# A fourth outer product done as inner products, in three of four pairs of the second matrix chain's first layer

## The chip, the core and the metric

The kernel runs on one core of one Trainium2 chip. The metric is the device time of one execution in microseconds (us); three runs of the kernel before gave 853.53, 854.23 and 855.94. A core has five engines that each work through their own list of instructions in order and wait for one another by semaphores: TensorE (PE in the profile; its weight loads are listed apart as PEld), VectorE (DVE), ScalarE (ACT), GpSimd (POOL) and SyncE (SP). SP, ACT and POOL also issue the transfers from and to memory. Matrix products land in PSUM, eight banks of 128 partitions by 512 fp32 columns; everything else is kept in SBUF.

## What is computed

```python
mask   = q_bucket[:, :, :, None] == k_bucket[:, :, None, :]      # 6 sign bits of q @ proj, k @ proj
scores = np.where(mask, scale * q @ k.T, -1e9)
x      = softmax(scores) @ v          # 4 batches x 8 heads x 768 x 64, laid out as 3072 x 512
h      = x @ w_in                     # 512 x 2048, "first layer"
g      = np.maximum(h, 0) ** 2        # gate
out    = g @ w_out                    # 2048 x 512, "second layer"; all fp32
```

## The kernel before

The attention comes first and fills `x` in memory (the first layer starts at 313.6 us in the trace). Then 3072 tokens go through the two layers in three chunks of 1024 (`i` = 0, 1, 2). For each chunk the *hidden stage* makes the gated hidden units and `project(i)` makes the output (the *output stage*). The order of all instructions is written out by hand (`tc.manual_schedule()`): what the code calls first stands first in each engine's queue.

Both layers use Strassen's scheme with seven products in place of eight (Winograd's form, with sums shared). `product` is one such level: `at(0..6)` are the seven left factors, `bt` the right ones, and the results c11, c12, c21, c22 come out of running sums in PSUM: products 0, 4, 5 and 2 are added one after the other into the same bank `acc0`, and after each of the first three ScalarE copies the running sum out (`one`, `two`, `three`) before the next may be added. Product 1 goes to a second bank, 3 and 6 to a third.

In chunk 0 the first layer is one level: for each of eight row blocks `r` of 128 hidden units, seven products of 128x512. In chunks 1 and 2 it is two levels, done in *pairs*: blocks `r0 = n` and `r = NQ + n` (n = 0 to 3) are made by two calls of `hidden_pair` (`half` 0 and 1). Four of the seven outer products (0, 3, 4, 5) are done plainly in each half, 128x512 each and two matmuls per product, by `add` (L1204 to L1210). The other three (1, 2, 6) are split once more: over the pair each is a set of seven inner products of 128x256, one matmul each. `inner_steps` gives such a set as four steps plus `put`; the sets are called A, B and C, and a set serves both blocks of the pair. The calls of `hidden_pair` set the order in which outer products and inner steps stand on TensorE. The copies out of PSUM are ScalarE's (`keep`, L1214, and L1166 to L1189), the sums of inner results VectorE's (L1169, L1183, L1185), `put` adds the outer partial result and gates (L1193, L1019), and `gate_sum` makes b22. Every matmul is fp32 and stands as two instructions in the trace.

After a pair VectorE forms differences of its gated blocks (`minus`, L676, `inner_sums`), which the output stage reads. The output stage is seven calls of `product` (k = 0 to 6), each seven products of 128x256 with four matmuls.

Transfers: `load_unit` loads a half's weights (`w_unit`, two buffers, 512 KB, SP's queue) two halves ahead; `load_inner` loads the inner factors of the next pair; `load_leaf` the second layer's factors on ScalarE's queue. `load_x(i + 1)` (2 MB, POOL's queue) stands at the start of the output stage. On the side ScalarE squares the raw q and k in 32 pieces (`peak`, 128x768, with a running sum) for a guard on the size of the scores; `load_peak(i + 2)` on POOL's queue fetches a piece two ahead into two buffers. Before, all 32 squares stand in the hidden stages of chunks 1 and 2, two in each half (`mark`).

In PSUM, `ps_m` has three names with two buffers each (`acc0` to `acc2`) and `ps_t` one tile of two banks (`spare`); its halves serve as the third bank `last` of the inner sets. In SBUF there are five buffers `h` (`new_h`), one `five`, two `one`, one `two`, two `three`, and two `o`, into which the output stage writes its results.

Of the kernel before, what the change touches and what calls it, by code (L numbers as in the profile page):

```python
# [34 lines left out]
def kernel(  # L35
# [10 lines left out]
    nc = tc.nc  # L46
# [51 lines left out]
    p_i = fast.enter_context(tc.tile_pool(name="p_i", bufs=2, side="right"))  # L98
    ps_t = fast.enter_context(tc.tile_pool(name="ps_t", bufs=1, space=PSUM))
    ps_s = first.enter_context(tc.tile_pool(name="ps_s", bufs=2, space=PSUM))  # L100
# [621 lines left out]
    def load_unit(n, pool=p_i):  # L722

        if n < NCHUNK * NR and n not in w_unit:
            r = order(n)
            w_unit[n] = pool.tile([P, 7, NFT // 2, P], FP32, name="w_unit", bufs=2 if pool is p_i else 1)
            m = 7 if n < NR else 4
            nc.sync.dma_start(out=w_unit[n][:, 0:m], in_=w_in_7[r, :, 0:m])

    def sum_x(i, n):  # L730
# [6 lines left out]
    with tc.manual_schedule():  # L737
# [182 lines left out]
        p_r = fast.enter_context(tc.tile_pool(name="p_r", bufs=2, reuse_waits="tile"))  # L920
        p_k = fast.enter_context(tc.tile_pool(name="p_k", bufs=1, reuse_waits="tile"))
        ps_m = fast.enter_context(tc.tile_pool(name="ps_m", bufs=2, space=PSUM, reuse_waits="tile"))
        HN, QN, NH = NCH // 2, NCH // 4, 5

# [7 lines left out]

        def product(n, w, at, bt, c11, c12, c21, c22, hook=None, last=False):

# [51 lines left out]
        def peak(i):  # L986

            t = raw_qk.pop(i)
            nc.scalar.activation(out=t, in_=t, func=ACTF.Square, accum_out=peaks[:, i:i + 1])

        top = p_k.tile([P, 1], FP32, name="top2")

# [3 lines left out]
        def guard():  # L996

            tp = spare("tp")[:, 0]
# [54 lines left out]

        w_inner, t_inner, snaps, now = {}, {}, {}, {}

# [70 lines left out]
        def quarters_x(i, j):  # L1126

            x = xs[i][0]
            b = (x[:, 2:4, 0:HN], x[:, 0:2, HN:NCH], x[:, 2:4, HN:NCH])[j]
            return b[:, 0, 0:QN], b[:, 0, QN:HN], b[:, 1, 0:QN], b[:, 1, QN:HN]  # L1130

        def sums_inner(i, js):

            for j in js:
                t = p_y.tile([P, NQ, QN], FP32, name=f"t{j}", **({"bufs": 2} if j < 2 else {}))
                t_inner.setdefault(i, {})[j] = t
                y11, y12, y21, y22 = quarters_x(i, j)
                minus(t[:, 0], y12, y11)
                minus(t[:, 1], y22, t[:, 0])
                minus(t[:, 2], y21, t[:, 1])  # L1140
                minus(y12, y22, y12)

        def inner_steps(i, n, j):


            w, t = w_inner[i, n][j], t_inner[i][j]
            y11, t3, y21, y22 = quarters_x(i, j)
            hs = {}
            if i not in snaps:
                o = [p_y.tile([P, HN], FP32, name="o", bufs=NOUT) for _ in range(2)]  # L1150
                o = [o[m // 2][:, m % 2 * QN:(m % 2 + 1) * QN] for m in range(3)]
                snaps[i] = o, [t_inner[i][m][:, 3] for m in range(3)], spare("acc3")
            side = (3 * n + (0, 2, 1)[j]) % 2
            one, two, five = snaps[i][side]
            three = one
            last = snaps[i][2][:, side, 0:QN]

# [5 lines left out]
            def step_0():  # L1163
                a0, a1 = (ps_m.tile([P, 512], FP32, name=f"acc{m}")[:, 0:QN] for m in (1, 2))
                mul(a0, 0, y11, True, False)
                nc.scalar.copy(out=one, in_=a0)  # L1166
                mul(a1, 1, y21, True, True)
                hs[0] = new_h()
                nc.vector.tensor_tensor(out=hs[0][:, 0:QN], in0=a1, in1=one, op=ALU.add)  # L1169
                hs["a0"] = a0  # L1170

            def step_1():
                hs["a2"] = last
                mul(hs["a0"], 4, t[:, 1], False, False)
                nc.scalar.copy(out=two, in_=hs["a0"])
                mul(hs["a2"], 3, t[:, 0], True, False)
                nc.scalar.copy(out=five, in_=hs["a2"])

            def step_2():
                mul(hs["a0"], 5, t3, False, False)  # L1180
                nc.scalar.copy(out=three, in_=hs["a0"])
                mul(hs["a2"], 6, y22, False, True)
                nc.vector.tensor_tensor(out=hs[0][:, QN:HN], in0=hs["a2"], in1=two, op=ALU.add)  # L1183
                hs[1] = new_h()
                nc.vector.tensor_tensor(out=hs[1][:, QN:HN], in0=three, in1=five, op=ALU.add)  # L1185

            def step_3():
                mul(hs["a0"], 2, t[:, 2], False, True)
                nc.scalar.copy(out=hs[1][:, 0:QN], in_=hs["a0"])  # L1189

            def put(unit, out, other):
                h = hs[unit]
                nc.vector.tensor_tensor(out=h, in0=h, in1=other, op=ALU.add)  # L1193
                gated(out, h)

            return step_0, step_1, step_2, step_3, put

        def hidden_pair(i, n, half):

            r0, r = n, half * NQ + n  # L1200
            w, bt = w_unit.pop(i * NR + 2 * n + half), factors_x(i)
# [10 lines left out]
            def keep(of, name):  # L1212
                t = p_r.tile([P, 512], FP32, name=name, bufs=KEPT[name])
                nc.scalar.copy(out=t, in_=of)  # L1214
                return t

            def mark(m):
                peak(2 * ((i - 1) * NR + 2 * n + half) + m)

            if half == 0:  # L1220
                load_inner(i, n + 1)
                load_third_inner(i, n + 1, nc.sync)
                now["A"], now["C"], now["B"] = (inner_steps(i, n, j) for j in range(3))
            A, B, C = (now[c] for c in "ABC")
            add(acc, 0, "11", True, False)
            one = keep(acc, "one")
            if half == 0:
                A[0]()
            else:
                B[2]()  # L1230
                C[0]()
                A[4](1, b11[:, r], one)
                B[4](0, b12[:, r0], now["two"])
            mark(0)
            other = ps_m.tile([P, 512], FP32, name="acc2")
# [11 lines left out]
            if half == 0:  # L1247
                A[2]()
                B[0]()
                A[4](0, b11[:, r], one)  # L1250
                nc.vector.tensor_tensor(out=two, in0=two, in1=five, op=ALU.add)
            else:
                C[2]()
                nc.vector.tensor_tensor(out=two, in0=two, in1=five, op=ALU.add)
# [4 lines left out]
            mark(1)  # L1259
            add(acc, 5, "t3", False, True)  # L1260
# [46 lines left out]
        def add_to(out, one, two):  # L1307
            nc.vector.tensor_tensor(out=out, in0=one, in1=two, op=ALU.add)  # L1308

        def whole(one, two):  # L1310

            if two is None:
                return one
            t = p_y.tile([P, QN], FP32, name="tmp", bufs=2)
            add_to(t, one, two)
            return t

# [50 lines left out]
        def project(i):  # L1368

            V, W, U, X = (p_y.tile([P, 4, QN], FP32, name=f"sum{n}") for n in range(4))  # L1370
            outs = {}

# [54 lines left out]
            for k in range(7):  # L1427
# [23 lines left out]
                def hook():  # L1451
                    y21 = b[:, NQ:NR, 0:QN]
                    minus(y21, y21, t2)
                    if k > 1 and src:
                        factor_units(k - 1, src)
# [10 lines left out]
                def a_with_load(m, k=k):  # L1466
# [7 lines left out]
                    lambda p: use(2, p, None), lambda *p: use(3, *p), hook,  # L1474
                    (i, k) == (NCHUNK - 1, 6),
                )
# [60 lines left out]
        for i in range(NCHUNK):  # L1537
            for s in range(NR):
# [3 lines left out]
                else:  # L1542
                    hidden_pair(i, s // 2, s % 2)
                if i == 0:
# [18 lines left out]
                if i == 0:  # L1563
                    minus(b12[:, r], b22[:, r], b12[:, r])
                for n in range(2):
                    m = 2 * ((i - 1) * NR + s) + n
                    if 2 <= m + 2 < NPK:
                        load_peak(m + 2)
            if i == NCHUNK - 1:
# [215 lines left out]
```

## Time and profile before

| what | value |
|---|---|
| runs | 853.53, 854.23, 855.94 us; median 854.23 |
| profiled execution | 853.06 us, its span 851.5 us |
| PE busy | 846.1 us, 99% of the span |
| DVE, ACT, POOL busy | 746.2, 401.2, 167.8 us |
| TensorE clock granted | 0.999 of full |
| hidden stage of chunk 1 | 494.58 to 586.09 us, output stage to 670.70 us |
| hidden stage of chunk 2 | 670.70 to 762.21 us, output stage to the end |

The profile is one execution on the chip. "Busy" counts instructions, not waits; matmuls are pipelined, so the start of one instruction to the start of the next, not its listed duration, is what it costs TensorE. In a timeline row the first number is the start, the second the duration of the merged group, and brackets give the engine's idle time before it and who ended it. A row of stretches gives each engine's busy time and its number of instructions in a stretch.

### The profile page before, as it was taken

To read this page: it belongs to the slowest core of one execution; us is meant where nothing else is said; L and a number is where in the kernel's file an instruction comes from. 1 tells how busy PE (TensorE), PEld (TensorE's weight loads), DVE (VectorE), ACT (ScalarE), POOL (GpSimd) and SP (SyncE) were. 2 spreads that over 40 slices of the span, in tenths; PEclk is the share of its full clock that TensorE was granted. 3 is DMA by queue.
4 is the path that set the end of the run, shared out by engine and by line. 5 is a ranking of instruction groups with operands and counts; after the bars stand their busy time and mean duration, and the time that the engine had idled before them with its cause. 6 is when DMAs were issued, how large, how long until landed. Compare 5 with 4: busy or idle time off the path is not lost.

```text
span 851.5 us, 17019 instructions
## 1 busy us (share of the span) xinstructions
PE 846.1 (99%) x6594; PEld 532.4 (63%) x6594; DVE 746.2 (88%) x1023; ACT 401.2 (47%) x749; POOL 167.8 (20%) x283
## 2 busy tenths in 40 slices
PE   9999999999999999999999999999999999999998
PEld 4444444444465444444788866567888765668886
DVE  4898999999999988988999968888988788889777
ACT  5887777878777752222111145553111355541111
POOL 1321121303221201643122122221000311200003
PEclk9999999999999999999999999999999999999999
DMA  9966999989996517999977975527657865335467
GB/s 193 201 120 139 185 186 204 204 173 226 267 236 186 177 49 267 324 319 303 335 242 236 275 200 189 177 97 286 191 159 195 181 231 178 123 121 157 141 174 146
DMA packets 234229, 170.14 MB, mean 200 GB/s; under 512 B 164840, under 2 KB 193328, under 8 KB 234144
## 3 DMA queue, kind: packets, MB, share of 16 engines
q1 hardware_dynamic: 194384, 87.78, 42.3%
q0 software_dynamic: 16512, 42.45, 15.9%
q10 hardware_dynamic: 23248, 38.78, 14.6%
q8 instruction: 53, 0.87, 0.4%
q14 instruction: 32, 0.26, 0.1%
HBM read 127.15 MB, written 41.16 MB: 198 GB/s over the span
## 4 chain that ended last, share of the span: by engine, by line
PE 99%; ACT 0%; DVE 0%; issue 0%; POOL 0%; POOLq 0%
PE acc L942 41%; PE st L478 18%; PE xo L532 15%; PE acc L1206 13%; PE acc L1159 9%; PE tot L589 1%; PE hash L396 1%; PE tp L342 0%; PE xo L371 0%; PE hash L406 0%; PE xo L406 0%; ACT e L484 0%; PE acc L1358 0%; DVE o L1308 0%; ACT h L1360 0%
## 5 line engine op out<-in xcount | busy, mean ns | idle before, releaser
L484 ACT ACTIVATE e<-st 128x768 f32<-128x768 f32 x192 | 155.6, 811 | 56.0 <-PE st L478 51.8
L532 PE MATMUL xo<-e,v_nat 64*64 64x385 f32 (+1 forms) x1520 | 156.0, 483 | 0.0
L942 PE MATMUL acc<-b,leaf 128*128 128x256 f32 x600 | 133.0, 379 | 0.0
L942 PEld LDWEIGHTS acc<-b,leaf 128*128 128x128 f32 x600 | 113.8, 190 | 16.1 <-issue 0.5
L478 PE MATMUL st<-feat 64*64 64x384 f32 x1056 | 108.6, 482 | 0.0
L444 POOL DMA_DIRECT2D bits<-signed x120 | 62.1, 522 | 196.9 <-ACT signed L433 195.1
L532 PEld LDWEIGHTS xo<-e,v_nat 64*64 64x64 f32 (+1 forms) x1520 | 56.9, 133 | 67.3 <-issue 54.8
L1206 PE MATMUL acc<-t_x,w_unit 128*128 128x512 f32 x192 | 90.8, 595 | 0.0
L942 PE MATMUL acc<-t,leaf 128*128 128x256 f32 x336 | 76.0, 379 | 0.0
L942 PEld LDWEIGHTS acc<-t,leaf 128*128 128x128 f32 x336 | 63.8, 190 | 8.9 <-issue 0.3
L1019 DVE SCALAR_TENSOR_TENSOR b<-h 128x512 f32<-128x512 f32 x96 | 65.7, 691 | 3.0
L478 PE MATMUL st<-bits 64*64 64x384 bf16 x768 | 65.2, 324 | 0.0
L520 DVE TENSOR_TENSOR total<-total,e 128x1536 f32<-128x1536 f32 x32 | 56.0, 1750 | 7.6 <-ACT e L484 6.8
L520 DVE TENSOR_TENSOR t_x<-t_x,e 128x1536 f32<-128x1536 f32 x32 | 55.7, 1742 | 3.9 <-ACT e L484 3.8
L942 PE MATMUL acc<-x,w_unit 128*128 128x512 f32 x128 | 56.5, 593 | 0.0
L478 PEld LDWEIGHTS st<-feat 64*64 64x64 f32 x1056 | 39.0, 133 | 26.4 <-issue 21.7
L949 ACT COPY two<-acc 128x256 f32<-128x256 f32 (+1 forms) x29 | 12.5, 431 | 88.0 <-PE acc L942 78.6
L942 PE MATMUL acc<-b_t,leaf 128*128 128x256 f32 x240 | 53.8, 379 | 0.0
L1206 PEld LDWEIGHTS acc<-t_x,w_unit 128*128 128x128 f32 x192 | 35.8, 190 | 26.7 <-issue 23.0
L1327 POOL DMA_DIRECT2D out_dram<-h x24 | 15.5, 655 | 181.5 <-DVE h L1322 181.5
L942 PEld LDWEIGHTS acc<-b_t,leaf 128*128 128x128 f32 x240 | 45.6, 190 | 6.2
L949 ACT COPY one<-acc 128x256 f32<-128x256 f32 (+1 forms) x29 | 12.5, 431 | 77.6 <-PE acc L942 58.4
(192 smaller groups left out, 1379.2 us busy)
## 6 DMA issues: line engine op xcount, KB each, us to landing
leaf<-w_out ACTq DMA_DIRECT2D x142, 256.0 KB, 3.1
raw<-in_moe_w_in_dram SPq DMA_DIRECT2D x8, 1024.0 KB, 6.4
raw<-in_moe_w_out_dram SPq DMA_DIRECT2D x8, 1024.0 KB, 7.4
w_unit<-w_in SPq DMA_DIRECT2D x16, 512.0 KB, 4.0
w_unit<-w_in SPq DMA_DIRECT2D x8, 896.0 KB, 8.9
w_out<-sums POOLq DMA_DIRECT2D x16, 448.0 KB, 7.7
v_nat<-in_v_dram SPq DMA_DIRECT2D x16, 384.0 KB, 5.1
x_all<-x_raw SPq DMA_DIRECT2D x16, 384.0 KB, 3.2
```

The source lines that it names most:

```text
L396: nc.tensor.matmul(out=banks[g * NR_B:(g + 1) * NR_B, h, 0:HS], lhsT=projs[rows, h * D:h * D + NR_B], rhs=feat[pr][rows, w, c * HS:(c + 1) ...
L444: nc.gpsimd.dma_start(out=t[h * D:h * D + NBITS + 1, w, c * HS:(c + 1) * HS], in_=signed[pr % 2][at:at + NBITS + 1, h],)
L478: nc.tensor.matmul(out=st[k * HK:(k + 1) * HK, h, 0:HS], lhsT=src[1][rows, key], rhs=src[0][rows, cut], start=first, stop=not first, skip_ ...
L484: nc.scalar.activation(out=key_of(pr, kt)[:, :, i, 0:HS], in_=st[:, :, 0:HS], func=ACTF.Exp, scale=scale)
L520: nc.vector.tensor_tensor(out=totals[pr], in0=totals[pr], in1=e, op=ALU.add)
L532: return nc.tensor.matmul(out=outs[pr][h * D:(h + 1) * D, c, 0:HS + 1], lhsT=nat[pr, "v_nat"][rows, h, kt * D:(kt + 1) * D], rhs=key_of(pr ...
L942: nc.tensor.matmul(out=acc[to], lhsT=a(i), rhs=b(i), start=first and i == 0, stop=last and i == n - 1, skip_group_check=True,)
L949: nc.scalar.copy(out=t, in_=acc[of])
L1019: nc.vector.scalar_tensor_tensor(out=out, in0=h, scalar=0.0, in1=h, op0=ALU.max, op1=ALU.mult)
L1159: nc.tensor.matmul(out=out, lhsT=w(a), rhs=b, start=start, stop=stop, skip_group_check=True)
L1206: nc.tensor.matmul(out=to, lhsT=w[:, PLACE[a], f], rhs=bt[b](f), start=first and f == 0, stop=last and f == NFT // 2 - 1, skip_group_check ...
L1327: queue.dma_start(out=out[at, m0 + a * 32:m0 + (a + 1) * 32].rearrange("(c i) j -> i c j", i=32), in_=ot[a * 32:(a + 1) * 32].rearrange("i ...
```

## The change

In the pairs n = 0, 1, 2 of chunks 1 and 2 `hidden_wide` takes the place of `hidden_pair`: outer product 3 ("t1") is no longer two outer products but a fourth inner set D. Its right side is `t_x[0]`, whose four sums are made once per chunk into the two buffers `o`; three of its seven left factors are loaded with the unit of the pair's first half (slot 4 gets a second, 128 KB load) and four are made from them by VectorE in slots 5 and 6 (`sum_unit`). D's results for the two blocks (`fives`) are added to `two` and `three`. ScalarE now writes inner partial sums straight into `h`, and VectorE adds to them there (`adds`). b22 is added by VectorE and gated by ScalarE in two passes (Relu, Square: `gate_b22`). The second block's share of a pair's closing work (`rest`) is put off into the next pair's first half. The pair n = 3 keeps `hidden_pair`, with the new inner steps. `last` has two tiles of one bank each (`side_bank`); `ps_t` is closed with the attention's pools. `two` of the first half and the output stage's two `tmp` share one tile. The squares stand 9 in the hidden stage of chunk 1, 14 in its output stage (two per `product`, in `hook` and `beside`) and 9 in the hidden stage of chunk 2.

```diff
@@ load_unit
             nc.sync.dma_start(out=w_unit[n][:, 0:m], in_=w_in_7[r, :, 0:m])
+            if wide(n):
+                nc.sync.dma_start(out=w_unit[n][:, 4], in_=w_in_7[NQ + r, :, PLACE[3]])
+    def wide(n):
+        return n >= NR and n % 2 == 0 and n % NR // 2 < NQ - 1
+    def own_factors(w):
+        a = PLACE[3]
+        return (w[:, a, 0], w[:, a, 1], w[:, 4, 1]) + tuple(w[:, 5 + n // 2, n % 2] for n in range(4))
+    def sum_unit(n):
+        if n < NCHUNK * NR and wide(n):
+            w = w_unit[n]
+            a11, a12, a22, *to = own_factors(w)
+            sums_a(a11, a12, w[:, 4, 0], a22, *to)
@@ product
             three = keep(0, "three")
+            if beside:
+                beside()
             add(2, at(6), bt["22"], False, True)
@@ inner_steps
             def step_1():
-                hs["a2"] = last
-                mul(hs["a0"], 4, t[:, 1], False, False)
-                nc.scalar.copy(out=two, in_=hs["a0"])
-                mul(hs["a2"], 3, t[:, 0], True, False)
-                nc.scalar.copy(out=five, in_=hs["a2"])
+                mul(hs["a0"], 4, t2, False, False)
+                nc.scalar.copy(out=hs[0][:, QN:HN], in_=hs["a0"])
+                mul(last, 3, t1, True, False)
+                hs[1] = new(1)
+                nc.scalar.copy(out=hs[1][:, QN:HN], in_=last)
             def step_2():
...
-                nc.vector.tensor_tensor(out=hs[0][:, QN:HN], in0=hs["a2"], in1=two, op=ALU.add)
-                hs[1] = new_h()
-                nc.vector.tensor_tensor(out=hs[1][:, QN:HN], in0=three, in1=five, op=ALU.add)
+            def adds():
+                for unit, by in (0, last), (1, three):
+                    add_in(hs[unit][:, QN:HN], by)
+        def gate_b22(r):
+            nc.scalar.activation(out=b22[:, r], in_=b22[:, r], func=ACTF.Relu)
+            nc.scalar.activation(out=b22[:, r], in_=b22[:, r], func=ACTF.Square)
+        def hidden_wide(i, n, half):
...
+            add(acc, 0, "11", True, False)
+            one = keep(acc, "one")
+            if half == 0:
+                A[0]()
+                D[0]()
+                for step in behind_pair:
+                    step()
+                behind_pair.clear()
+            else:
+                B, C = inner_steps(i, 2, 0, w_inner[i, n][2]), inner_steps(i, 1, 1, w_inner[i, n][1])
+                B[0]()
+                C[0]()
+                B[1]()
+                gate_b22(r0)
+                A[4](1, b11[:, r], one)
+                sum_unit(i * NR + 2 * n + 2)
+            add(acc, 4, "t2", False, False)
+            two = keep(acc, "two")
+            if half == 0:
+                A[1]()
+                D[1]()
+            else:
+                B[2]()
+                C[1]()
+                B[3]()
+                C[2]()
+                mark()
+                B[5]()
+                B[4](0, b12[:, r0], now["two"])
+                add_in(two, fives[1])
+                C[5]()
+                B[4](1, b12[:, r], two)
+            add(acc, 5, "t3", False, True)
+            three = keep(acc, "three")
+            if half == 0:
+                A[2]()
+                D[2]()
+                A[3]()
+                D[3]()
+                mark()
+                A[5]()
+                D[5]()
+                A[4](0, b11[:, r0], one)
+                add_in(two, fives[0])
+                nc.vector.tensor_tensor(out=b22[:, r0], in0=three, in1=fives[0], op=ALU.add)
+                now["two"], now["three"] = two, three
+            else:
+                C[3]()
+                nc.vector.tensor_tensor(out=b22[:, r], in0=three, in1=fives[1], op=ALU.add)
+                C[4](0, b21[:, r0], now["three"])
+                def rest():
+                    gate_b22(r)
+                    C[4](1, b21[:, r], three)
+                    for m in r0, r:
+                        minus(b_t[:, m], b12[:, m], b11[:, m])
+                    inner_sums(0, slice(n, n + 1))
+                    for m in r0, r:
+                        minus(b12[:, m], b22[:, m], b12[:, m])
+                behind_pair.append(rest)
@@ project
                 if k == 2 and more:
                     sum_x(i + 1, 1)
                     sum_x(i + 1, 2)
+                    sum_unit((i + 1) * NR)
@@ project, hook
                     minus(y21, y21, t2)
+                    if i == 1:
+                        mark()
```

More of the change, by code (lines that the diff above doesn't have):

```diff
@@ L1134, in sums_inner, with inner_steps, new @@
             for j in js:
-                t = p_y.tile([P, NQ, QN], FP32, name=f"t{j}", **({"bufs": 2} if j < 2 else {}))
-                t_inner.setdefault(i, {})[j] = t
                 y11, y12, y21, y22 = quarters_x(i, j)
[L1138 to L1147, printed above, removed]
-            hs = {}
[L1149 to L1156, printed above, removed]
+                if j < 3:
+                    tile = p_y.tile([P, NQ, QN], FP32, name=f"t{j}", **({"bufs": 2} if j < 2 else {}))
+                    t = [tile[:, m] for m in range(NQ - 1)] + [y12]
+                    spots[i, j] = tile[:, NQ - 1]
+                else:
+                    pair = [p_y.tile([P, HN], FP32, name="o", bufs=NOUT) for _ in range(2)]
+                    t = [o[:, m * QN:(m + 1) * QN] for o in pair for m in range(2)]
+                t_inner[i, j] = t
+                minus(t[0], y12, y11)
+                minus(t[1], y22, t[0])
+                minus(t[2], y21, t[1])
+                minus(t[3], y22, y12)
+        def inner_steps(i, j, side, w):
+            t1, t2, t4, t3 = t_inner[i, j]
+            y11, _, y21, y22 = quarters_x(i, j)
+            if i not in snaps:
+                snaps[i] = [side_bank(m)[:, 0:QN] for m in range(2)]
+            one = three = spots[i, side]
+            last = snaps[i][side]
+            hs = {}
+            def new(unit):
+                if j == 3 and unit == 0:
+                    return p_r.tile([P, 512], FP32, name="five", bufs=KEPT["five"])
+                return new_h()
             def mul(out, a, b, start, stop):
@@ L1224, in hidden_pair @@
+        def hidden_pair(i, n, half):
+            r0, r = n, half * NQ + n
+            w, acc, add, keep = outer_steps(i, n, half)
+            if half == 0:
+                now["A"], now["C"], now["B"] = (
+                    inner_steps(i, j, (0, 0, 1)[j], w_inner[i, n][j]) for j in range(3)
+                )
             A, B, C = (now[c] for c in "ABC")
@@ L1228, in hidden_pair @@
                 A[0]()
+                for step in behind_pair:
+                    step()
+                behind_pair.clear()
             else:
                 B[2]()
+                B[5]()
                 C[0]()
@@ L1313, in whole @@
                 return one
-            t = p_y.tile([P, QN], FP32, name="tmp", bufs=2)
-            add_to(t, one, two)
-            return t
+            turns.reverse()
+            add_to(turns[0], one, two)
+            return turns[0]
         def put_out(i, ih, jh, n, o):
```

80 lines of the change are left out of this document (51 added, 29 removed).

## The prediction

> **What bounds the kernel now.** First the page: the span, the engines' shares, and the chain of work that ended last.
>
> ```profile
> span 851.5 us, 17019 instructions
> PE 846.1 (99%) x6594; PEld 532.4 (63%) x6594; DVE 746.2 (88%) x1023; ACT 401.2 (47%) x749; POOL 167.8 (20%) x283
> ...
> PE 99%; ACT 0%; DVE 0%; issue 0%; POOL 0%; POOLq 0%
> PE acc L942 41%; PE st L478 18%; PE xo L532 15%; PE acc L1206 13%; PE acc L1159 9%; PE tot L589 1%; PE hash L396 1%; PE tp L342 0%; PE xo L371 0%; PE hash L406 0%; PE xo L406 0%; ACT e L484 0%; PE acc L1358 0%; DVE o L1308 0%; ACT h L1360 0%
> ```
>
> The chain is TensorE from end to end; the changed stages are the 22% of L1206 and L1159. Next, busy time by stretches, one for each pair (columns: stretch and length, then PE, PEld, DVE, ACT and POOL, each busy and number of instructions, then clock, DMA share, GB/s).
>
> ```profile
> 494.58:517.46 22.88, 22.88 (x75) 13.98 (x74) 14.79 (x29) 12.30 (x30) 4.15 (x8) 1.00 0.61 171
> 517.46:540.34 22.88, 22.88 (x76) 13.98 (x74) 18.96 (x35) 12.83 (x32) 4.26 (x9) 1.00 0.51 175
> ...
> 739.34:762.20 22.86, 22.86 (x75) 13.97 (x74) 18.94 (x35) 12.71 (x32) 2.67 (x5) 1.00 0.40 133
> ```
>
> A pair takes 22.88 us, all of it TensorE at full clock, while DVE has 3.9 us and ACT 10 us to spare. So time can be won only by fewer matmul columns, and lost only by making TensorE wait. What a matmul costs is read from starts, in TensorE's timeline of the second pair:
>
> ```profile
> 517.46 1.88 PE L1206 MATMUL acc<-x,w_unit 128*128 128x512 f32 x4
> 519.18 1.03 PE L1159 MATMUL acc<-x,sum 128*128 128x256 f32 x4
> 520.04 1.88 PE L1206 MATMUL acc<-t_x,w_unit 128*128 128x512 f32 x4
> ...
> 538.11 1.96 PE L1206 MATMUL acc<-t_x,w_unit 128*128 128x512 f32 x4
> 539.91 0.59 PE L1159 MATMUL acc<-t,sum 128*128 128x256 f32 x2
> 540.34 1.88 PE L1206 MATMUL acc<-x,w_unit 128*128 128x512 f32 x4
> ```
>
> Four instructions (two fp32 matmuls) of 512 columns take 519.18 - 517.46 = 1.72, so 0.86 us for each matmul; of 256 columns 520.04 - 519.18 = 0.86, so 0.43. At 538.11 the group needs 1.80 in place of 1.72: 0.08 lost once a pair, where only one inner step (0.86) stands between two outer products of one bank and the copy `two` comes late. Check: 16 x 0.86 + 21 x 0.43 + 0.08 = 22.87.
>
> **The change, part by part.**
>
> *Matmuls.* Each of six pairs drops four 512-wide matmuls (4 x 0.86 = 3.44) and gains seven 256-wide ones (7 x 0.43 = 3.01): -0.43. Between outer products on one bank now stand 1.72 us of inner steps or more, so the 0.08 goes too. A wide pair: 12 x 0.86 + 28 x 0.43 = 22.36, that is -0.51; six of them **-3.1 us**. The price of a 256-wide matmul is a row of this very stage, so I take it; the bounds are the rivals'.
>
> *Hand-overs through PSUM.* From the queues, TensorE in a wide first half is at 0 outer, 1.72 A0, 2.58 D0, 3.44 outer, 5.16 A1, 6.02 D1, 6.88 outer, 8.60 A2, 9.46 D2, 10.32 A3, 10.75 D3, end 11.18; in the second 0 outer, 1.72 B0, 2.58 C0, 3.44 B1, 4.30 outer, 6.02 B2, 6.88 C1, 7.74 B3, 8.17 C2, 9.03 outer, 10.75 C3. The shortest distance from a running sum to the next addition on it is 1.29 (D2 to D3, C1 to C2). What it needs:
>
> ```profile
> 508.78 1.03 PE L1159 MATMUL acc<-x,sum 128*128 128x256 f32 x4
> ...
> 509.41 0.37 ACT L1166 COPY o<-acc 128x256 f32<-128x256 f32 x1 [0.44 <-PE acc L1159]
> ...
> 537.45 0.59 ACT L1214 COPY two<-acc 128x512 f32<-128x512 f32 x1 [1.34 <-PE acc L1206]
> ```
>
> Matmul start to copied: 509.78 - 508.78 = 1.00; end of a copy to the waiting matmul: 538.04 to 538.11 + 0.08 = 0.15. Together 1.15 of 1.29: no stall, 0.14 in hand. Bounds: 0 to 0.2 at each of three such places a pair (late by another short copy, 0.37 - 0.14), 18 places, 0 to +3.6; I take 0.
>
> *VectorE and ScalarE.* Groups of the second and third pair (mean in ns at the end of the busy column):
>
> ```profile
> L1019 DVE SCALAR_TENSOR_TENSOR b<-h 128x512 f32<-128x512 f32 x16 | 11.1, 692 | 0.6
> L1183 DVE TENSOR_TENSOR h<-acc,o 128x256 f32<-128x256 f32 x3 | 1.3, 425 | 3.1 <-PE acc L1159 3.1
> L989 ACT ACTIVATE raw_qk<-raw_qk 128x768 f32<-128x768 f32 x8 | 6.8, 853 | 0.0
> L1214 ACT COPY one<-acc 128x512 f32<-128x512 f32 x4 | 2.3, 586 | 5.3 <-PE acc L1206 5.3
> L989 ACT ACTIVATION_READ_ACCUMULATOR raw_qk<-raw_qk 128x1 f32 x8 | 1.6, 198 | 0.0
> L1181 ACT COPY o<-acc 128x256 f32<-128x256 f32 x3 | 1.1, 376 | 0.1
> ```
>
> DVE gains three 256-wide adds net (3 x 0.43), loses b22's two gates (2 x 0.69) and gets `sum_unit`, four 128-wide operations that no row shows: between 0 and 4 x 0.43. So 18.96 + 1.3 - 1.4 + 0 to 1.7 = 18.9 to 20.6 of 22.36. ACT gains five short copies (1.9) and four passes of Relu and Square (0.59 to 0.85 each), loses two long copies (1.2) and two squares with their reads (2.1): 12.8 + 1.0 to 2.0, about 14.3. Both stay under TensorE. `rest`, some 5 us of DVE, moves into the next first half; nothing on TensorE waits for it before the output stage, only ACT's gate and the `h` buffers, whose next writers stand half a pair on. Chunk start: D's sums, four 256-wide DVE operations (1.7 us), with 4.5 us idle to hide in; in the output stage `sum_unit` meets idle time as well:
>
> ```profile
> 497.59 0.39 DVE L1169 TENSOR_TENSOR h<-acc,o 128x256 f32<-128x256 f32 x1
> 502.52 0.42 DVE L1183 TENSOR_TENSOR h<-acc,o 128x256 f32<-128x256 f32 x1 [4.55 <-PE acc L1159]
> ```
> ```profile
> 437.81 1.22 DVE L676 TENSOR_TENSOR b_t<-b_t,t 128x1024 f32<-128x1024 f32 x1 [0.64 <-PE acc L942]
> 439.63 0.42 DVE L670 TENSOR_TENSOR h<-h 128x256 f32<-128x256 f32 x1 [0.60 <-DMA h<-w_in]
> ```
>
> D1 needs its sums at 494.58 + 6.02 = 500.6; they are done by 498.0 + 1.7 = 499.7. Cost 0.
>
> *Buffers.* `tmp` shared with `two`, `last` as two tiles, `ps_t` closed with the attention: no instruction and no bank more, cost 0. New is that ACT, not DVE, is the first to write some `h` buffers at a chunk's start (A1, D1: 500 to 502 us), and so waits for the output stage's transfers out of them. The last on POOL's queue:
>
> ```profile
> 489.50 2.57 POOL L1327 DMA_DIRECT2D out_dram<-h  x4 [1.54 <-DVE h L1322]
> ```
> ```profile
> out_dram<-h POOLq DMA_DIRECT2D x4, 64.0 KB, 4.4
> ```
>
> Landed by 492.1 + 4.4 = 496.5, so 0; were ACT held there, `three` and then the sums behind it would be late next.
>
> *Loads.* SP issues six more transfers (0.3 us each, behind `load_unit`); the two for unit 2n + 2 go out when D3 frees its buffer.
>
> ```profile
> L728 SPq DMA_DIRECT2D w_unit<-w_in x8: 319/319/320, 505.1 to 585.9; - x8
> ...
> DMA to landing us min/median/max: 3.7/3.9/6.4
> ```
>
> Landed 4.5 to 7.3 us into the second half (0.8 for the issues). `sum_unit` waits for that on DVE, from about 5.4 us on (behind two adds at B0 and C0 and A's put and gate). Behind it in DVE's queue stand four 256-wide adds, five 512-wide adds and gates and b22: 4 x 0.43 + 6 x 0.69 = 5.9, plus itself 0 to 1.7; behind b22 on ACT Relu, Square (1.2 to 1.7) and `two` (0.59), and for `two`, 0.15 later, TensorE's third outer product of the next half at 11.18 + 6.88 = 18.06. Latest harmless landing: 18.06 - 5.9 - 2.4 - (0 to 1.7) less up to 0.5, so 7.5 to 9.8, middle 8.7. Cost 0.
>
> *Squares in the output stage.* 14 x (0.85 + 0.20) = 14.7 us on an ACT that has room:
>
> ```profile
> 579.50:662.00 82.50, 82.50 (x374) 70.71 (x373) 74.23 (x104) 14.24 (x38) 3.42 (x6) 1.00 0.64 199
> ```
> ```profile
> 600.11 0.37 ACT L949 COPY one<-acc 128x256 f32<-128x256 f32 x1 [1.35 <-PE acc L942]
> ...
> 603.56 0.37 ACT L949 COPY two<-acc 128x256 f32<-128x256 f32 x1 [3.08 <-PE acc L942]
> ```
> ```profile
> 586.48 0.75 POOL L713 DMA_DIRECT2D x<-x_all  x1 [0.22 <-PE acc L1159]
> ```
> ```profile
> x<-x_all POOLq DMA_DIRECT2D x1, 2048.0 KB, 12.2
> ```
> ```profile
> raw_qk<-in_q_dram POOLq DMA_DIRECT2D x16, 192.0 KB, 2.7
> raw_qk<-in_k_dram POOLq DMA_DIRECT2D x16, 192.0 KB, 4.2
> ```
> ```profile
> 605.09 5.34 PE L942 MATMUL acc<-b,leaf 128*128 128x256 f32 x24
> ```
>
> A square fits the 3.08 us hole before `two`. The tight one is the first of k = 1: its piece is fetched behind x on POOL's queue, which lands at 586.48 + 12.2 = 598.7; 2.7 to 4.2 more give 601.4 to 602.9, then 1.05 of square and 0.37 of `two`: 604.3 at the latest, and TensorE adds on that bank at 605.09. Cost 0, with two pieces sharing the rate up to 2 us.
>
> **Sum**: -3.1 us. The profiled execution took 853.06 (span 851.5 and 1.56 around it) and becomes 850.0; the median of the three runs is 1.2 above it, so the forecast is **851.1**, -0.36%. By matmuls alone (-2.6) it is 851.6.
>
> **Rivals.**
>
> 1. *The unit lands late* (the one on the slower side). At four places (n = 0, 1 of two chunks) each us past 8.7 stalls TensorE for one. From 9.5 the gain is gone (4 x 0.8), from 10.1 the kernel is over 0.3% slower: 857. For it: DVE has not waited for a transfer there before. Against: 6.4 is the longest of eight.
> 2. *Tight hand-overs*: up to +3.6 against -3.1: 852 to 854.7, no change. For it: 0.14 us of margin and more small work on ACT; against: ACT is 36% idle.
> 3. *A square waits for its piece*: up to +2 once, so 851.6 to 853, mostly within 0.3%.
> 4. *Narrow matmuls cost more than half.* Weight loads are 190 ns for each pass whatever the width:
>
> ```profile
> L1159 PEld LDWEIGHTS acc<-x,sum x128: 190/190/190, 495.9 to 759.6; 128*128 128x128 f32 x128
> L1159 PE MATMUL acc<-x,sum x128: 379/379/379, 496.3 to 759.8; 128*128 128x256 f32 x128
> ```
> If durations (379 and 592 ns) ruled, a pair would gain 14 x 0.379 - 8 x 0.592 = +0.57, six +3.4: 857.7. Against: starts are 215 ns apart, above 190. The Trainium skill, "TensorE: Matmul & The Clock Gate", section "Back-to-back issue gap", speaks for it: it puts streams of weight loads and matmuls at about 81 ns for 128 columns and 131 ns for 512, so that four times the columns cost far less than four times the time. On that rule the change would lose (an estimate on a straight line: 0.75 of a wide matmul in place of half, +6.4 us in all); the rows above, 0.43 against 0.86, disagree.
> 5. *DVE falls behind*: needs 1.8 us a pair above the 20.6; each us beyond costs six: 857 from 2.7.
>
> **Chances.** Forecast 0.58; rival 1 0.07, 2 0.16, 3 0.10, 4 0.03, 5 0.06. A measurement of this kernel tells about 0.3% (2.6 us) from no change; the forecast lies only 0.5 beyond. Faster: 0.58 less a twentieth, and a little of 3: 0.57. Same: most of 2 and 3, and that twentieth: 0.26. Slower: 1, 4, 5 and the top of 2: 0.17. The range goes from 850.0 (the lowest run, 853.53, less 3.1, and 0.4 of scatter) to 857.0, where rivals 1, 4 and 5 begin; the forecast's own is 850.0 to 852.2.
>
> **What would show it.** Right: pairs of 22.4 us in TensorE's timeline, the 1.96 group gone from the wide pairs, the output stage of chunk 1 still 84.6 us without PE idle, DVE 19 to 20.6 us a pair. Wrong: TensorE idle before an outer product released by ACT `two` behind Relu (rival 1 or 5), idle of tenths before D3 or C2 (2), one gap near k = 1 (3), 256-wide starts over 0.43 apart (4).

## The result and the profile after

The changed kernel takes 851.88 us (median of 7 runs, 851.42 to 852.57), the kernel before in the same comparison 854.23 (7 runs, 853.41 to 855.94): a ratio of 0.9973 with a 95% interval of 0.9961 to 0.9984. The forecast was 851.1, a ratio of 0.9963. A second comparison, with 10 runs of the changed kernel and 32 of the one before, gave 0.9979 (0.9970 to 0.9989).

First the page of the changed kernel: span and engines' shares.

```profile
span 850.9 us, 17227 instructions
PE 844.0 (99%) x6630; PEld 543.6 (64%) x6630; DVE 750.3 (88%) x1061; ACT 420.2 (49%) x791; POOL 167.9 (20%) x283
```

The span is only 0.6 us shorter than before, less than the runs say, because this execution was slower where no code changed: its first layer begins at 314.76 us instead of 313.56, and from TensorE's last instruction to the end it takes 4.7 us instead of 3.9. (Over the profiles of the changed kernel and its edits the first layer begins between 312.8 and 314.8 us, with nothing edited ahead of it.) So the change is read from its own stages. These are the four pairs and the output stage of chunk 1, then the first pair of chunk 2, by stretches (columns as in the prediction):

```profile
495.61:518.26 22.65, 22.64 (x81) 15.11 (x80) 16.09 (x37) 12.35 (x31) 1.99 (x4) 1.00 0.52 142
518.26:540.65 22.39, 22.39 (x81) 15.20 (x80) 19.37 (x41) 14.36 (x35) 2.14 (x5) 1.00 0.46 150
540.65:563.04 22.39, 22.39 (x82) 15.20 (x81) 18.30 (x36) 14.36 (x35) 2.13 (x5) 1.00 0.45 145
563.04:585.91 22.87, 22.87 (x75) 13.98 (x74) 19.09 (x35) 13.04 (x32) 3.21 (x7) 1.00 0.47 161
585.91:670.52 84.61, 84.61 (x393) 74.48 (x392) 77.78 (x117) 24.20 (x60) 21.05 (x38) 1.00 0.86 260
670.52:693.20 22.68, 22.67 (x82) 15.13 (x81) 16.22 (x37) 12.27 (x31) 1.96 (x4) 1.00 0.64 179
```

The pairs n = 1 and 2 take 22.39 us, where 22.36 was forecast; n = 3, which keeps its form, 22.87; the output stage 84.61, as before. But n = 0 takes 22.65, and 22.68 in chunk 2: some 0.28 too long, twice. The two hidden stages fell from 91.51 to 90.30 and 90.32: 2.4 us, and that is what the runs show. TensorE's timeline of the pair n = 0 shows where the 0.28 lies:

```profile
513.68 0.59 PE L1204 MATMUL acc<-t,sum 128*128 128x256 f32 x2
514.12 0.59 PE L1204 MATMUL last<-t,sum 128*128 128x256 f32 x2
514.72 0.70 PE L1204 MATMUL acc<-t,leaf 128*128 128x256 f32 x2
515.25 0.59 PE L1204 MATMUL acc<-x,sum 128*128 128x256 f32 x2
```

A group of two takes 0.43 from start to start; here it is 0.60 and 0.53. The group at 514.72 is B3, the addition behind the copy of B2's running sum. ScalarE's timeline leads from there to the cause:

```profile
510.87 0.37 ACT L1219 COPY h<-acc 128x256 f32<-128x256 f32 x1 [0.49 <-PE acc L1204]
512.36 0.37 ACT L1222 COPY h<-last 128x256 f32<-128x256 f32 x1 [1.11 <-DVE b L1056]
512.62 0.63 ACT L1249 ACTIVATE b<-b 128x512 f32<-128x512 f32 x1
513.29 0.63 ACT L1250 ACTIVATE b<-b 128x512 f32<-128x512 f32 x1
513.82 0.57 ACT L1271 COPY two<-acc 128x512 f32<-128x512 f32 x1
514.29 0.38 ACT L1226 COPY t<-acc 128x256 f32<-128x256 f32 x1
...
533.96 0.37 ACT L1222 COPY h<-last 128x256 f32<-128x256 f32 x1
534.23 0.63 ACT L1249 ACTIVATE b<-b 128x512 f32<-128x512 f32 x1
```

B1's copy into `h` (L1222) waits 1.11 us for a gate of VectorE; in the pair n = 1 (533.96) it waits for nothing. Behind it stand Relu and Square of b22, `two`, and the copy that B3 needs (514.29, done at 514.67). The gate is that of A's second result, and VectorE's timeline has it at the same place in both pairs, ended 16.6 and 16.7 us into them:

```profile
511.55 0.69 DVE L1056 SCALAR_TENSOR_TENSOR b<-h 128x512 f32<-128x512 f32 x1
...
534.23 0.69 DVE L1056 SCALAR_TENSOR_TENSOR b<-h 128x512 f32<-128x512 f32 x1
```

VectorE is no later in n = 0. So the copy must have been given another buffer than in n = 1. Of the five `h`, one still belonged to the last output tile of the stage before, whose transfers SP issues late (issues on SP's queue, start and length; the eight are those of the last two tiles, four each):

```profile
496.87 4.17 SPq L1471 DMA_DIRECT2D out_dram<-h  x8
```

Hence the theory: where the pool hands out buffers (in the program's order) that tile is still in use when C0 asks, C0 gets the buffer of A's first result, and B1 the next one, A's second.

### The profile page after: what moved, and what is told of

It reads as the page before. It is cut to its first block, busy times and chain, and to the rows that moved or that the text cites. A ratio compares the mean times of both kernels' runs of the same rounds, so it can differ in the third digit from the quotient of the medians.

```text
span 850.9 us, 17227 instructions
## 1 busy us (share of the span) xinstructions
PE 844.0 (99%) x6630; PEld 543.6 (64%) x6630; DVE 750.3 (88%) x1061; ACT 420.2 (49%) x791; POOL 167.9 (20%) x283
## 4 chain that ended last, share of the span: by engine, by line
PE 96%; DMA 2%; DVE 1%; issue 0%; ACT 0%; POOL 0%; SPq 0%; ACTq 0%; POOLq 0%; DVEq 0%
PE acc L967 40%; PE st L478 18%; PE xo L532 14%; PE acc L1260 11%; PE acc L1204 8%; PE last L1204 3%; PE tot L589 1%; PE hash L396 1%; DMA bits<-signed 1%; DMA out_dram<-h 1%; PE tp L342 0%; DMA qk_nat<-in_q_dram 0%; DVE h L1466 0%; DVE o L1450 0%; PE hash L406 0%
## 5 line engine op out<-in xcount | busy, mean ns | idle before, releaser
L532 PEld LDWEIGHTS xo<-e,v_nat 64*64 64x64 f32 (+1 forms) x1520 | 58.7, 133 | 65.5 <-issue 54.7
L1260 PE MATMUL acc<-t_x,w_unit 128*128 128x512 f32 x144 | 67.8, 593 | 0.0
L1056 DVE SCALAR_TENSOR_TENSOR b<-h 128x512 f32<-128x512 f32 x84 | 57.4, 691 | 2.6
L1011 POOL DMA_DIRECT2D raw_qk<-in_q_dram x32 | 17.3, 541 | 211.2 <-ACT raw_qk L1016 194.8
L478 PE MATMUL st<-t_x 64*64 64x384 f32 x480 | 48.9, 482 | 0.0
```

What stands on the lines that cost most here:

```text
L478: nc.tensor.matmul(out=st[k * HK:(k + 1) * HK, h, 0:HS], lhsT=src[1][rows, key], rhs=src[0][rows, cut], start=first, stop=not first, skip_ ...
L532: return nc.tensor.matmul(out=outs[pr][h * D:(h + 1) * D, c, 0:HS + 1], lhsT=nat[pr, "v_nat"][rows, h, kt * D:(kt + 1) * D], rhs=key_of(pr ...
L1011: nc.gpsimd.dma_start(out=raw_qk[i][:, w], in_=flat[:, i * n:(i + 1) * n])
L1056: nc.vector.scalar_tensor_tensor(out=out, in0=h, scalar=0.0, in1=h, op0=ALU.max, op1=ALU.mult)
L1260: nc.tensor.matmul(out=to, lhsT=w[:, PLACE[a], f], rhs=bt[b](f), start=first and f == 0, stop=last and f == NFT // 2 - 1, skip_group_check ...
```

## The experiments

All of them are edits of the changed kernel. Stage lengths are from TensorE's timelines; "end" is from TensorE's last start to the end of the span.

| run | hidden 1 | output 1 | hidden 2 | end | median us |
|---|---|---|---|---|---|
| kernel before | 91.51 | 84.61 | 91.51 | 3.9 | 853.4 |
| after_again | 90.32 | 84.60 | 90.32 | 4.8 | 852.01 |
| last_tile_pool | 90.04 | 84.61 | 90.03 | 5.0 | 852.11 |
| gate_dve | 90.27 | 84.61 | 90.27 | 3.6 | 850.68 |
| squares_back | 90.32 | 84.60 | 90.32 | 4.5 | 851.71 |
| d3_first | 91.21 | 84.60 | 91.21 | 4.7 | 853.36 |
| four_wide | 90.11 | 87.10 | 90.02 | 6.6 | 857.64 |
| four_wide_pool | 89.84 | 87.09 | 89.80 | 6.8 | 857.04 |
| four_wide_2 | 89.55 | 84.83 | 89.54 | 6.9 | 852.75 |
| four_wide_3 | 89.55 | 85.34 | 89.54 | 6.4 | 853.10 |
| late_unit | 96.60 | 84.60 | 95.83 | 4.3 | 874.14 |
| act_16 | 90.31 | 84.61 | 90.31 | 4.2 | 851.20 |
| pe_8 | 90.32 | 84.60 | 90.32 | 7.0 | 855.15 |

The kernel before was 853.2 to 853.4 in each of the later comparisons. The medians scatter by about 1 us with nothing changed in a stage; the stage lengths repeat within 0.03.

**after_again**, the changed kernel unedited.

> The changed kernel once more, unedited, so that the runs beside it are compared on the same chip. Expected 851.9, pair n = 0 of chunks 1 and 2 with 0.27 us of idle before B3.

Measured: 852.01 (0.9979 of before, 0.9970 to 0.9989), and the same 0.28 us before and behind B3 in both first pairs.

**last_tile_pool**: the buffer comes back in time.

```diff
-queue = nc.gpsimd if (ih, jh) == (1, 1) else nc.sync
+queue = nc.gpsimd if (ih, jh) == (1, 1) or (ih, jh, n) == (1, 0, 1) else nc.sync
```

> The changed kernel with one edit: in chunks 0 and 1 the last output tile of the output stage is written out by POOL's queue instead of SP's, so that its buffer h is released before the next chunk's first pair asks for its sixth h. Theory (rotation of h): in pair n = 0 the copy of B1 (h<-last, L1222) has waited 1.1 us for the gate of A's second result, behind it Relu, Square, two and three, and B3 has come 0.27 late; with the buffer back in turn B1 waits for the gate of A's first result, which is long over. Pair n = 0 becomes 22.39 us as n = 1 and 2 are (it was 22.65), in chunks 1 and 2: 0.27 + 0.27, so 851.9 becomes 851.3. Rival (VectorE is behind at the chunk's start because of the four sums for D): the edit leaves VectorE's work as it is, the pair stays 22.65 and the time 851.9.

Measured: the hidden stages fall by 0.28 and 0.29. ScalarE's timeline, where the same copy now stands without a wait:

```profile
510.14 0.37 ACT L1219 COPY h<-acc 128x256 f32<-128x256 f32 x1 [0.49 <-PE acc L1204]
510.57 0.37 ACT L1222 COPY h<-last 128x256 f32<-128x256 f32 x1
510.84 0.63 ACT L1249 ACTIVATE b<-b 128x512 f32<-128x512 f32 x1
```

The rival, VectorE's backlog, falls: its work was left as it is. The median, 852.11, does not show the 0.57; that is below what it can show. The hand-out of buffers is shown by what the edit undoes, not by a row that names a buffer.

**gate_dve**: b22's gate on VectorE, as in the kernel before.

```diff
-nc.scalar.activation(out=b22[:, r], in_=b22[:, r], func=ACTF.Relu)
-nc.scalar.activation(out=b22[:, r], in_=b22[:, r], func=ACTF.Square)
+gated(b22[:, r], b22[:, r])
```

> The changed kernel with b22's gate back on VectorE, one instruction in place of Relu and Square on ScalarE. Theory (rotation of h): the 1.1 us wait of B1's copy in pair n = 0 stays, but 1.2 us of ScalarE work between it and two is gone, so B3 is no longer late and pair n = 0 is 22.39; VectorE goes from 19.4 to 20.8 us of 22.4 a pair, which still fits: 851.3. Rival (VectorE falls behind): its order is full where b12 and two are added, and outer products wait for ScalarE copies into buffers that VectorE still reads: idle of some tenths in every wide pair, 852 to 854.

Measured: 850.68 (0.9973, 0.9958 to 0.9988), which overlaps the changed kernel's interval. The wide pairs stay free of idle, so VectorE does not fall behind; but n = 0 keeps 0.24 us, a miss of the theory's detail. ScalarE's timeline:

```profile
512.14 0.37 ACT L1222 COPY h<-last 128x256 f32<-128x256 f32 x1 [1.71 <-DVE b L1056]
512.41 0.59 ACT L1270 COPY two<-acc 128x512 f32<-128x512 f32 x1
```

On VectorE the gate of b22 stands ahead of A's second result, so the same buffer comes free 0.6 us later: B1's copy waits 1.71 instead of 1.11 and now holds B2's addition on `last` itself (0.24), not B3. The wait for the buffer is the root in both; the gate on ScalarE only sets which matmul it reaches.

**squares_back**: all squares in the hidden stages again, two in place of one at each `mark` of `hidden_wide`, one more in `hidden_pair`, none in `project`.

> The changed kernel with all 32 squares in the hidden stages again: two instead of one at each of the two places in a wide pair's halves, none in the output stage. Theory (a copy behind the second square comes late): in half 0 the second square ends near 2.7 us into the next half, the copy of B0 ends at 3.6 to 3.8 and B1, due at 3.44, comes 0.3 to 0.5 late: 6 x 0.4 = 2.4, so 854.3. Rival (ScalarE has 8 us of idle in each pair, the place of a square does not matter): 851.9.

Measured: 851.71, no idle added, ScalarE at 15.9 us a pair. The theory fell: two squares side by side take 1.76 us from the first start to the last end, not 2.1, because the next square starts while the sum of the one before is read, so B0's copy ends 3.0 us into the half and B1 is due at 3.44. ScalarE's timeline, at the end of a first half (the next half begins at 528.81):

```profile
529.28 0.85 ACT L1016 ACTIVATE raw_qk<-raw_qk 128x768 f32<-128x768 f32 x1
530.02 0.20 ACT L1016 ACTIVATION_READ_ACCUMULATOR raw_qk<-raw_qk 128x1 f32 x1
530.12 0.83 ACT L1016 ACTIVATE raw_qk<-raw_qk 128x768 f32<-128x768 f32 x1
530.85 0.19 ACT L1016 ACTIVATION_READ_ACCUMULATOR raw_qk<-raw_qk 128x1 f32 x1
```

Moving squares to the output stage costs nothing and here buys nothing.

**d3_first**: what a hand-over needs.

```diff
 A[2]()
 D[2]()
-A[3]()
 D[3]()
+A[3]()
 mark()
```

> The changed kernel with A3 and D3 exchanged, so that D3 follows D2 after 0.86 us instead of 1.29. Theory (a hand-over needs 1.00 from the start of the matmul pair to the end of the copy, and 0.15 from there to the next addition, 1.15): 0.29 of idle before D3 in each wide pair, 6 x 0.29 = 1.7, so 853.6. Rival (the hand-over needs less, the order does not matter): 851.9; if it needs more than 1.29, idle stood there before and grows by 0.43 a pair: 854.5.

Measured: 853.36; each hidden stage 0.89 us longer, that is 0.30 a wide pair. TensorE's timeline of the second pair:

```profile
526.72 0.59 PE L1204 MATMUL acc<-o,w_unit 128*128 128x256 f32 x2
527.15 0.59 PE L1204 MATMUL last<-t_x,w_unit 128*128 128x256 f32 x2
527.77 0.70 PE L1204 MATMUL acc<-o,w_unit 128*128 128x256 f32 x2
528.31 0.59 PE L1204 MATMUL acc<-t,sum 128*128 128x256 f32 x2
```

D2 at 526.72, D3 at 527.77 and stretched by 0.1: 0.30 of idle where 1.15 less 0.86 gives 0.29. The margin of 0.14 us in the changed kernel's order is real, and it is enough.

**late_unit**: the unit's load three times over, each behind the one before (`for _ in range(3 if wide(n) else 1)` around the load in `load_unit`).

> The changed kernel with the main load of every wide pair's first unit issued three times one behind the other, each waiting for the one ahead of it. The unit, whose landing has been bounded by 5.4 us into the second half, then lands after three issues and landings of 0.3 and 3.8 us, near 12.5. Theory (the prediction's latest harmless landing, 7.5 to 9.8, middle 8.7, and from there a us for a us at four places): 3.8 x 4 = 15 us more (11 to 20), 867 (863 to 872), the idle ahead of the third outer product of the next pair's first half or of an inner sum ahead of it. Rival (VectorE's order has more room than that sum says): under 5 us more, 852 to 857.

Measured: 874.14 (2 runs), outside both. In the profiled execution 13.4 us of the loss lie at the start of chunk 0's output stage, a side effect of the edit that I had not counted: SP's queue was held there, and leaves for the output stage stood behind it (one wait of 10.7 us for `leaf`). The four places of the prediction lost 3.2, 3.1, 3.5 and 2.0 us, 11.8 in all. First VectorE's timeline at the first of them, then TensorE's:

```profile
533.43 0.29 DVE L670 TENSOR_TENSOR w_unit<-w_unit 128x128 f32<-128x128 f32 x1 [7.94 <-DMA w_unit<-w_in]
```
```profile
520.04 1.88 PE L1261 MATMUL acc<-x,w_unit 128*128 128x512 f32 x4
...
533.10 1.99 PE L1261 MATMUL acc<-x,w_unit 128*128 128x512 f32 x4 [1.43 <-DMA w_unit<-w_in]
...
541.50 1.98 PE L1261 MATMUL acc<-t_x,w_unit 128*128 128x512 f32 x4 [1.25 <-ACT tmp L1272]
```

The unit landed 13.4 us into the second half (520.04). From there to the third outer product of the next half passed 541.50 - 533.43 = 8.07, so the latest harmless landing is 18.06 - 8.07 = 10.0, just above the 7.5 to 9.8 of the prediction. The matmul that waits and its releaser (ScalarE's first-half copy, now `tmp`) are those of rival 1; half of the loss falls earlier, on the first outer product, which needs the unit itself at 11.18.

**four_wide** and **four_wide_pool**: the pair n = 3 in the wide way (with `wide` and the call of `sum_unit` to match); the second also has last_tile_pool's edit.

```diff
-(hidden_wide if s // 2 < NQ - 1 else hidden_pair)(i, s // 2, s % 2)
+hidden_wide(i, s // 2, s % 2)
...
 B[4](1, b12[:, r], two)
+if n == NQ - 1:
+    mark()
+    for m in r0, r:
+        minus(b_t[:, m], b12[:, m], b11[:, m])
+    inner_sums(0, slice(n, n + 1))
...
-behind_pair.append(rest)
+if n < NQ - 1:
+    behind_pair.append(rest)
+else:
+    rest()
```

> The changed kernel with the pair n = 3 done in the wide way too; its closing work (differences for b_t, the sums of the first output product) stands in the second half and right behind it instead of in a next pair. Theory: the last pair of chunks 1 and 2 goes from 22.87 to 22.39 us, 2 x 0.48 = 1.0: 851.9 becomes 850.9. Rival (the output stage begins late): the sums of b11 that its third product reads (3.4 us after its start) are the last of some 4 us of VectorE work behind B's second gate; each is late by tenths to 1 us, and the time is 851 to 852.5.

> Both edits together, four wide pairs and the last output tile on POOL's queue. If the two gains are apart from each other: four pairs of 22.39 in both chunks, 851.9 - 1.0 - 0.5 = 850.4. If the output stage begins late, the loss of the run with four wide pairs alone stands here too, 850.5 to 852.

Measured: 857.64 (1.0051, 1.0037 to 1.0066) and 857.04, beyond the rival. TensorE stops at the start of both output stages. ScalarE's timeline of four_wide, then TensorE's:

```profile
588.22 0.63 ACT L1249 ACTIVATE b<-b 128x512 f32<-128x512 f32 x1 [2.92 <-DVE b L1344]
588.88 0.63 ACT L1250 ACTIVATE b<-b 128x512 f32<-128x512 f32 x1
...
589.42 0.35 ACT L974 COPY one<-acc 128x256 f32<-128x256 f32 x1
```
```profile
584.67 3.62 PE L967 MATMUL acc<-b,leaf 128*128 128x256 f32 x16
589.82 2.43 PE L967 MATMUL acc<-t,leaf 128*128 128x256 f32 x10 [1.53 <-ACT one L974]
```

Not the sums were late but the copy `one`: it stands behind the gate of b22 on ScalarE, and the gate waited 2.92 us for VectorE. Of the 2.5 us that the first output stage lost, 1.7 lie here; the other 0.8 lie in the next 13 us, where one row waits for a leaf's transfer (0.17 us, at 595.45) and the rest was not traced further. This is the danger that the prediction named for a wait on ScalarE, in another place.

**four_wide_2** is four_wide_pool with that set right: `rest` of n = 3 runs in the `hook` of the first output product, behind `one`; the leaves at the end of the hidden stage are loaded on SP's queue. What each of the two edits gave was not taken apart.

> Four wide pairs and the last output tile on POOL's queue, as before, with two more edits: the closing work of n = 3 (the gate of b22 on ScalarE first) stands behind the first copy of the output stage instead of ahead of it, and the five leaf loads at the end of the hidden stage are issued by SP instead of ScalarE. Theory (the output stage began late because ScalarE, with the copy `one` of the first output product behind it, waited 2.9 us for b22's sum in VectorE's queue): the 1.7 us of idle at the output stage's start and the 0.3 before B1 go, all pairs are 22.39: 851.9 - 1.0 - 0.5 = 850.4. Rival (VectorE's sums for the output stage are themselves late): idle of 1 to 2 us stays ahead of the output stage's second and third product, 854 to 856.

Measured: all pairs 22.39, hidden stages 89.55 and 89.54, the 1.7 gone, 0.2 left in the output stage. Yet the median is 852.75, 0.7 above after_again: 1.55 gained in the hidden stages, 0.2 given back in the output stage and 2.1 at the end of the span, behind TensorE's last instruction, where no edit lies. The profile of that end has one block more on the instruction queue. The next three runs ask whose.

**four_wide_3** is four_wide_2 with gate_dve's edit (32 instructions fewer on ScalarE).

> The run with four wide pairs that mended the output stage's start, and b22's gate on VectorE in place of ScalarE, which takes some twenty instructions off ScalarE's program. That run had hidden stages of 89.55 us (90.31 in the changed kernel) and still was no faster: from TensorE's last instruction to the end of the span passed 6.9 us in place of 4.7, with one fetch on the instruction queue more (54, before 53), the last thing before the end. Theory (the longer program of ScalarE crosses into one more block of code, fetched at the very end): 53 fetches again, some 4.7 us at the end, hidden stages 89.6 to 89.8, so 850.2. Rival (the block is TensorE's, whose program stays as it is): 54 fetches, 6.9 us at the end, 852.5.

Measured: the rival. 54 blocks, an end of 6.4 us, 853.10; its output stage of chunk 1 is also 0.7 us longer than the changed kernel's.

**act_16**: 16 small copies more on ScalarE.

```diff
+if i == 0 and k in (2, 4):
+    spot = p_k.tile([P, 16], FP32, name="spot")
+    for m in range(8):
+        nc.scalar.copy(out=spot, in_=ident[:, 0:16])
```

> The changed kernel with 16 copies of 16 columns more on ScalarE, eight each in two output products of chunk 0, where ScalarE is idle for several us at a time; they change no result and nothing reads them. Theory (a block of ScalarE's code more): 54 fetches instead of 53, the end 2 us longer, 854.0. Rival (not ScalarE's program): 53 fetches and 851.9.

Measured: the rival again, 53 blocks, 851.20.

**pe_8**: eight small transposes more on TensorE.

```diff
+if i == 0 and k == 4:
+    tp = side_bank(0)
+    for m in range(8):
+        nc.tensor.transpose(out=tp[0:1, 0:P], in_=ident[:, 0:1], identity=ident)
```

> The changed kernel with eight small transposes more on TensorE in one output product of chunk 0 (identity columns into an unused bank; nothing reads them). The runs with four wide pairs had eight to twelve TensorE instructions more than the changed kernel, one fetch more on the instruction queue and some 2 us more at the end; neither fewer nor more instructions on ScalarE moved that. Theory (TensorE's program crosses into one more block of code): 54 fetches, 6.5 to 7 us from TensorE's last instruction to the end in place of 4.2 to 4.9, and with 0.5 to 1 us for the transposes 854.0 to 855.0. Rival (the fetch comes from something else in the four wide pairs): 53 fetches, 852.0 to 852.8.

Measured: 855.15, 3.1 above after_again: 0.87 for the transposes, 2.2 at the end. The page of pe_8, with the queue's row (blocks, MB, share), and then that of the changed kernel:

```profile
span 853.8 us, 17239 instructions
PE 845.0 (99%) x6638; PEld 544.2 (64%) x6638; DVE 750.3 (88%) x1061; ACT 420.2 (49%) x791; POOL 167.7 (20%) x283
...
q8 instruction: 54, 0.88, 0.4%
```
```profile
q8 instruction: 53, 0.87, 0.4%
```

Eight transposes on TensorE alone, far from the end of the program, bring the 54th block and the longer end.

## Why the prediction was right, and the term that it missed

*Matmuls: right.* Wide pairs without idle take 22.39 against 22.36, and the group of 1.96 us is gone from them. Rival 4 is refuted by the pairs themselves: seven narrow matmuls for four wide ones gain 0.43, as the spacing of the starts said, and not the durations. The spacing that the Trainium skill, "TensorE: Matmul & The Clock Gate", section "Back-to-back issue gap", gives for streams of weight loads and matmuls (81 ns at 128 columns, 131 ns at 512) does not carry over to these fp32 matmuls: by the prediction's estimate from it the change would have lost 6.4 us, and the stages gained 2.4.

*Hand-overs: right.* No idle before D3 or C2; d3_first puts the need at 1.16 (0.86 and the 0.30 lost) against the 1.15 worked out from two rows.

*VectorE and ScalarE: right in that both fit.* VectorE takes 19.4 us in n = 1, of a forecast 18.9 to 20.6, and 18.3 in n = 2, below the forecast (no `sum_unit` stands there, and the rest was put 0.6 too high); ScalarE 14.4 of 14.3.

*Buffers: the step that failed.* It said "Landed by 492.1 + 4.4 = 496.5, so 0", from the last transfer on POOL's queue, and it looked for the wait at A1 and D1; it came at B1, and for a gate of VectorE. SP's transfers out of another `h` are issued until 501.0. By the theory above, what matters is not when the data has left, since C1 would ask for that buffer only at 514.8, but that in the program's order it was not free when C0 asked, so that the later requests got other buffers. The cost is 0.28 us a chunk, 0.57 in all; last_tile_pool shows it, and that it hangs on that tile's queue. With it the sum is -2.5, and the stages show -2.4.

*Loads: right.* `sum_unit` ran at 512.16, right behind the gate ahead of it, with no wait; the margin reaches to 10.0 rather than 8.7, so rival 1 was a little less near than thought.

*Squares: right,* output stage 84.61. The tight one, the first of k = 1, ran at 600.38, its piece landed at least 1 us before the estimate. squares_back shows that the move was not needed for the time.

*The sum.* -3.1 forecast, -2.4 in the stages: the difference is the 0.57 of the buffers and 0.02 in each wide pair (22.88 became 22.39, a gain of 0.49 for the 0.51 forecast). The medians say -2.35 in the first comparison but only -1.36 in the second (853.37 to 852.01), where an end of 4.8 us for 3.9 takes part of the gain. That the first comes so near the stages is therefore luck in part, and so is the nearness of 851.88 to 851.1: the forecast starts from a median of 854.23 before, and in the later comparisons the kernel before took 853.2 to 853.4.

## What to carry to other kernels

Price a swap of wide for narrow matmuls by the spacing of starts in the same stage, and the hand-over between running sums by the copy's end plus the restart; both held here within hundredths of a us. When another engine becomes the first to write a rotating buffer, ask who held each buffer last in the program's order, not only when its data left: a wait there moves all that is queued behind it. And read a small gain from the stages: their lengths repeat within 0.03 us, the medians of these runs scatter by about 1.

## What the runs showed of the hardware

The queue that the page calls q8 instruction brings blocks of 16 KB (0.87 MB in 53 packets). Eight more transposes on TensorE, with their weight loads, brought one more block, and with it a longer end. In pe_8 the last 6 us of the span show two single bursts after the output has gone, each of about 16 KB (40 slices of 0.15 us, GB/s):

```profile
GB/s 92 135 112 132 143 273 81 35 282 164 7 55 17 10 0 0 109 0 0 0 0 0 0 0 0 0 0 0 0 0 0 0 0 0 0 0 0 109 0 0
```

The same view of after_again has one such burst. The queue's row in these 6 us, of pe_8 and then of after_again:

```profile
q8 instruction: 2, 0.03, 2.0%
```
```profile
q8 instruction: 1, 0.02, 1.4%
```

So it is in every profile: two blocks in the last 6 us where the page has 54, one where it has 53. The end takes 3.6 to 5.0 us in the runs with 53 blocks and 6.4 to 7.0 in the five with 54; the difference, some 2 us, is more than a fourth wide pair gains in both chunks (2 x 0.48). The change itself, with 36 matmul instructions more, stayed under the edge by less than these eight. What at the end waits for the block, no row says. A version with four wide pairs and twelve matmul instructions saved elsewhere has as many as the changed kernel (6630 of 6642) and would, as an estimate from the ends of these runs, take some 2 us less than four_wide_2; it was not tried.
